# Turning the attention probabilities of eight token tiles by four 128x128 transposes each, with v laid out key by key

## The chip, the cores and the metric

The kernel runs on one core of a Trainium2 chip. The metric is device time in microseconds of one execution. Five engines work side by side, each through its own list of instructions in order: TensorE (PE: matrix products and transposes into PSUM), VectorE (DVE), ScalarE (ACT), GpSimd (POOL) and SyncE (SP), which here only issues DMAs. An engine that must wait for another's result holds up everything behind it in its list.

## The reference

Two steps on 4608 tokens. Attention inside chunks of 64 tokens, for 8 batches, 8 heads of 64 features and 9 chunks per sequence of 576:

```python
scores = scale * np.matmul(q_c, k_c.transpose(0, 1, 2, 4, 3))
scores = scores - np.max(scores, axis=-1, keepdims=True)
attn = np.exp(scores)
attn = attn / (np.sum(attn, axis=-1, keepdims=True) + 1e-09)
out = np.matmul(attn, v_c)
```

The heads of a token are then laid side by side to 512 features x, and

```python
h = x @ w_in                      # 512 -> 2048
g = np.where(h > 0.0, h, np.exp(np.minimum(h, 0.0)) - 1.0)
return g @ w_out                  # 2048 -> 512
```

The weights `w_in` and `w_out` arrive as float64 and are rebuilt on the chip into a high and a low part, so that three products of reduced precision stand for one product of full precision.

## The kernel before, in words

Tokens are worked in blocks of 512, a block in four token tiles of 128. A token tile is two chunks of 64 tokens, c = 0 and 1, on the 128 partitions. The first three blocks ("plain") use weights held on the chip; the remaining six go in pairs with fewer products, ordered by a planner, and the change does not touch them.

Attention of the first eight token tiles goes through `early_attention` (line 264), a generator whose steps other work is put between: q and k of the tile are transposed on PE in four 128x128 pieces each (L270) and copied to SBUF by ACT (L277); 16 small products per tile give the scores (L248), each on a 64x64 quarter of the array; DVE takes the maximum per head (L283) and subtracts it (L299), ACT takes exp (L303), DVE sums and divides (L305 to L308). Three of the eight tiles (2, 4 and 5, `BY_HEAD`) have exp and sum on ACT head by head instead (L293). Then the probabilities `a` (128 tokens by 8 heads of 64 keys) must be turned so that keys lie on partitions: before, 16 matmuls against 64x64 corners of the identity, one per head and chunk (L315). ACT copies the result (L322) and 16 small products with v give x (L256). Half of the array serves chunk 0, half chunk 1: `v_sb` holds the 64 tokens of chunk 0 on partitions 0 to 63 with all 8 heads, and of chunk 1 on partitions 64 to 127. One DMA loads it (`load_heads`, L206), or two where the tile's chunks belong to two batches (tile 4).

Tiles 0 to 3 are worked ahead of everything by a written list of items, `START`: `q0`, `k0`, `v0` are loads, `u0`, `u1`, ... loads of a weight unit (`load_unit`, L118 and L125; a unit u is 128 columns of `w_in` and, from u1 on, 128 rows of `w_out`), `0` to `3` the next step of that tile, `r` and `d` steps of the rebuilding of a unit on ACT (L139, L144, L179) and DVE (L161, L168, L172, L185). Units arrive in three buffers `st`. Tiles 4 to 7 are worked inside the first block by a second list, `FIRST_BLOCK`, between its 16 rounds: `H` is 12 products into `h` (L434; L451 in the first round), `e` the steps of the elu (ACT L468, L469, L476; DVE L471, L479), `P` 12 products into `o`, `L4` to `L7` the loads of a token tile and `4` to `7` its steps. The rebuilding of units 3 to 16 runs in the same list, so DVE and ACT rebuild the weights just ahead of the products that use them.

SP issues every load in the order of these lists. The framework gives DMAs eight semaphores in turn, and a DMA waits until the eighth DMA before it has landed.

Of the kernel before, what the change touches and what calls it, by code (L numbers as in the profile page):

```python
# [10 lines left out]
F32 = mybir.dt.float32  # L11
# [4 lines left out]
ALU = mybir.AluOpType  # L16
# [4 lines left out]
def kernel(  # L21
# [181 lines left out]
    def load_heads(src, name: str, n0: int, pool):  # L203
# [4 lines left out]
            )  # L208
        return dst

    U = 4

    def load_tokens(n0: int, qk):
# [39 lines left out]
    def multiply_v(x_ps, v_sb, aT):  # L253
        for hp in range(NK):
            for c, j in quarters:
                nc.tensor.matmul(  # L256
                    x_ps[halves[j], c, hp, :], lhsT=v_sb[halves[c], 2 * hp + j, :],
                    rhs=aT[halves[c], :, j * NK + hp], start=True, stop=True,
                )

    def first_halves(pair_of_banks):
        return pair_of_banks[:, :, :NK * C].rearrange("p i (h t) -> p i h t", h=NK)

    def early_attention(tt: int, q_sb, k_sb, get_v, kT, at, a_pool, get_banks, put, by_head: bool):


        both = get_banks()
        for i, src in enumerate((q_sb, k_sb)):
            for hp in range(NK):
                nc.tensor.transpose(  # L270
                    out=both[:, i, hp * P:(hp + 1) * P], in_=src[:, 2 * hp:2 * hp + 2, :],
                    identity=ident,
                )
# [11 lines left out]
        a_heads = a.rearrange("p (j h) t -> p j h t", j=2)  # L285
        z = sm.tile([P, 2, NK, 1], F32, name="z")
        if by_head:

            nc.vector.tensor_scalar_mul(mx, mx, -SCALE)
            yield  # L290
            for j in range(2):
                for h in range(NK):
                    nc.scalar.activation(  # L293
                        out=a_heads[:, j, h, :], in_=scores[:, j, h, :], func=AF.Exp, scale=SCALE,
                        bias=mx[:, j, h, :], accum_out=z[:, j, h, :],
                    )
            yield
        else:
            nc.vector.tensor_tensor(  # L299
                out=a_heads, in0=scores, in1=mx.broadcast_to([P, 2, NK, C]), op=ALU.subtract  # L300
            )
            yield
            nc.scalar.activation(out=a, in_=a, func=AF.Exp, scale=SCALE)  # L303
            yield
            nc.vector.tensor_reduce(out=z, in_=a_heads, axis=AX.X, op=ALU.add)  # L305
        nc.vector.tensor_scalar_add(z, z, 1e-9)
        nc.vector.reciprocal(z, z)
        nc.vector.tensor_tensor(  # L308
            out=a_heads, in0=a_heads, in1=z.broadcast_to([P, 2, NK, C]), op=ALU.mult
        )  # L310
        yield
        turned_ps = both[:, 0, :].rearrange("p (h t) -> p h t", h=H)
        for h in range(H):
            for half in halves:
                nc.tensor.matmul(  # L315
                    turned_ps[half, h, :], lhsT=a[half, h, :], rhs=ident[half, half],
                    start=True, stop=True,
                )
        yield

        aT = at.tile([P, NK, P], F32, name="qT").rearrange("p h (j t) -> p (h j) t", j=2)
# [92 lines left out]
    def by_chunk(x, ts):  # L414
        return x[:, :, ts].rearrange("p h (c t) -> p c h t", c=2)

    def keep_x(n: int, src):
        half = (n // NTT + 1) % 2 if n >= PLAIN * NTT else 0
        ts = slice(n % NTT * P, (n % NTT + 1) * P)
        nc.scalar.copy(out=by_chunk(xf[:, half], ts), in_=src)  # L420

    def split_first_x(tt: int, src):
        ts = slice(tt * P, (tt + 1) * P)
        hi = by_chunk(xhi, ts)
        nc.scalar.copy(out=hi, in_=src)
        nc.vector.tensor_tensor(
            out=by_chunk(xlo, ts), in0=src, in1=hi.bitcast(F32), op=ALU.subtract)

# [698 lines left out]
    with (  # L1127
        tc.tile_pool(name="start", bufs=NTT) as start,
        tc.tile_pool(name="ps_start", bufs=NTT, space=bass.MemoryType.PSUM) as ps_start,
    ):  # L1130
        make_identity(nc, ident)
        loaded, tiles, warmed = {}, {}, []

        def start_banks():
            return ps_start.tile([P, 2, DM], F32, name="ps_a")

        def start_step(item: str):
            tt = int(item)
            if tt not in tiles:
                tiles[tt] = early_attention(  # L1140
                    tt, *[loaded[kind, tt] for kind in "qk"], lambda: loaded["v", tt],
                    start.tile([P, NK, P], F32, name="kT"), start, start,
                    lambda: start_banks() if tt else warmed[0],
                    split_first_x, tt in BY_HEAD)
            next(tiles[tt])

        for item in START.split():
            kind, n = item[0], item[1:]
            if kind == "w":
                warm(int(n))  # L1150
            elif kind == "u":
                load_unit(int(n))
            elif kind in "qkv":
                loaded[kind, int(n)] = load_heads(
                    {"q": q, "k": k, "v": v}[kind], f"{kind}_sb", int(n) * P, start)
# [31 lines left out]
    def early_tile(n: int):  # L1187

        n0 = n * P
        heads = [io[:, 2 * (n % 2) + i, :].rearrange("p (h d) -> p h d", h=H) for i in range(2)]  # L1190
        loaded = [load_heads(src, name, n0, pool)
                  for src, name, pool in ((q, "q_sb", heads[0]), (k, "k_sb", heads[1]), (v, "v_sb", vio))]
        q_sb, k_sb, v_sb = loaded
        return early_attention(
            n % NTT, q_sb, k_sb, lambda: v_sb, k_turned, at, wi1,
            lambda: ps_early.tile([P, 2, DM], F32, name="ps_a"),
            lambda tt, src: keep_x(tt, src), n in BY_HEAD)

    def place_of_tokens(n: int):

# [744 lines left out]
```

## Time and profile before

| | us |
|---|---|
| median of 3 runs (lowest, highest) | 826.16 (824.86, 826.62) |
| span of the profiled execution, first to last instruction | 823.4 |
| what lies around the span, median less span | 2.8 |

| engine | busy us | share of the span |
|---|---|---|
| PE | 804.4 | 98% |
| DVE | 613.1 | 74% |
| ACT | 523.5 | 64% |
| POOL | 171.1 | 21% |

The profiled execution has no time of its own beside its span; the median of the runs stands for it. Busy shares are averages over stages with different limits. The stage before the first product of the first block lasts 28.9 us, the first block about 100 us, and what the change does lies in these two. A duration in a row includes a little of the next instruction's start, so the distance between the starts of two rows in a row is the cost of the first.

### The profile page before, as it was taken

The numbers are of one execution on the slowest core, as the hardware profiler recorded it, in microseconds if no ns is written. First come the engines' busy times: TensorE is split into PE (matmuls) and PEld (weight loads), VectorE is DVE, ScalarE is ACT, GpSimd is POOL, SyncE is SP. The second block draws the span as 40 slices with busy tenths as digits, with TensorE's granted clock in tenths as the row PEclk, the third lists the DMA queues.
The fourth block names the chain that finished last, engine by engine and source line by source line (L and its number), as shares of the span: only waits on it lengthen the run. The fifth ranks groups of instructions, "written<-read, shape, count | busy, mean of one in ns | idle before, by whom it ended". The sixth has DMA issues, their size and how long they took to land.

```text
span 823.4 us, 15851 instructions
## 1 busy us (share of the span) xinstructions
PE 804.4 (98%) x5853; PEld 655.6 (80%) x5853; DVE 613.1 (74%) x914; ACT 523.5 (64%) x990; POOL 171.1 (21%) x149
## 2 busy tenths in 40 slices
PE   6799999999999999999999999999999999999997
PEld 5688878888778878878888888778788888888885
DVE  4999997666776659767656867868889956557964
ACT  5999885544554546766666445888867737776451
POOL 0000014264525531443111254000020100000100
PEclk9999999999999999999999999999999999999999
DMA  9976994889778887689986789999876585566755
GB/s 234 272 212 209 270 328 130 244 243 267 219 215 231 231 269 205 202 241 281 283 235 188 218 246 299 286 322 287 249 204 206 195 269 193 193 196 190 226 186 149
DMA packets 183229, 191.90 MB, mean 233 GB/s; under 512 B 84720, under 2 KB 151792, under 8 KB 183152
## 3 DMA queue, kind: packets, MB, share of 16 engines
q1 hardware_dynamic: 182512, 188.80, 77.2%
q0 software_dynamic: 640, 2.10, 0.6%
q8 instruction: 46, 0.75, 0.4%
q14 instruction: 31, 0.25, 0.1%
HBM read 144.18 MB, written 42.99 MB: 227 GB/s over the span
## 4 chain that ended last, share of the span: by engine, by line
PE 83%; DMA 8%; SPq 3%; ACT 2%; DVE 2%; issue 1%; DVEq 0%; ACTq 0%
PE o L434 43%; PE h L434 34%; DMA ring<-a_dram 3%; PE ps_a L248 2%; PE ps_a L256 2%; SPq L206 2%; PE h L451 1%; DMA st<-in_moe_w_out_dram 1%; DMA kept<-in_k_dram 1%; DMA a_dram<-wi_lo 1%; DMA kept<-in_q_dram 1%; DMA a_dram<-wi_hi 1%; DMA v_sb<-in_v_dram 1%; PE ps_a L315 1%; DMA ring<-w_dram 1%
## 5 line engine op out<-in xcount | busy, mean ns | idle before, releaser
L434 PE MATMUL o<-wo_hi,ghi 128*128 128x512 f32 x272 | 107.6, 396 | 0.0
L434 PE MATMUL o<-wo_hi,glo 128*128 128x512 f32 x272 | 106.1, 390 | 0.3 <-DVE glo L479 0.3
L434 PE MATMUL o<-wo_lo,ghi 128*128 128x512 f32 x272 | 106.0, 390 | 0.0
L434 PE MATMUL h<-xhi,wi_hi 128*128 128x512 f32 x228 | 84.0, 397 | 0.1
L434 PE MATMUL h<-xlo,wi_hi 128*128 128x512 f32 x228 | 82.3, 390 | 0.0
L434 PE MATMUL h<-xhi,wi_lo 128*128 128x512 f32 x180 | 70.3, 390 | 0.0
L434 PEld LDWEIGHTS o<-wo_hi,glo 128*128 128x128 f32 x272 | 51.1, 188 | 11.7 <-DVE glo L479 0.7
L434 PEld LDWEIGHTS o<-wo_hi,ghi 128*128 128x128 f32 x272 | 51.0, 188 | 11.1
L434 PEld LDWEIGHTS o<-wo_lo,ghi 128*128 128x128 f32 x272 | 51.1, 188 | 10.2
L510 POOL TENSOR_TENSOR kept<-wi_hi,wi_lo 128x512 f32<-128x512 f32 x16 | 21.7, 1376 | 158.8 <-DVE xf L172 118.2
L471 DVE SCALAR_TENSOR_TENSOR e<-e,h 128x512 f32<-128x512 f32 x48 | 32.8, 684 | 25.2 <-ACT e L469 24.8
L434 PE MATMUL o<-split,ring 128*128 128x512 f32 x216 | 51.0, 390 | 0.0
L434 PEld LDWEIGHTS h<-xhi,wi_hi 128*128 128x128 f32 x228 | 42.6, 188 | 9.8 <-ACT kept L785 0.8
L434 PEld LDWEIGHTS h<-xlo,wi_hi 128*128 128x128 f32 x228 | 42.8, 188 | 8.5
L434 PEld LDWEIGHTS o<-split,ring 128*128 128x128 f32 x216 | 40.5, 188 | 8.4
L393 ACT COPY unturned<-turned 128x512 f32<-128x512 f32 x28 | 17.4, 621 | 46.0 <-DVE turned L388 37.9
L468 ACT ACTIVATE e<-h 128x512 f32<-128x512 f32 x48 | 28.6, 596 | 25.0 <-PE h L434 22.5
L476 ACT CAST ghi<-e 128x512 fp32r<-128x512 f32 x48 | 29.8, 621 | 19.8 <-DVE e L471 19.6
L746 POOL TENSOR_TENSOR glo<-e,ghi 128x512 fp32r<-128x512 f32 x16 | 20.7, 1296 | 96.9 <-ACT ghi L744 96.9
L434 PE MATMUL h<-split,ring 128*128 128x512 f32 x168 | 40.3, 391 | 0.0
L1492 ACT ACTIVATE e<-e 128x512 f32<-128x512 f32 x64 | 39.5, 630 | 1.0
L434 PEld LDWEIGHTS h<-xhi,wi_lo 128*128 128x128 f32 x180 | 33.8, 188 | 7.5 <-DVE wi_lo L185 0.4
(225 smaller groups left out, 2011.3 us busy)
## 6 DMA issues: line engine op xcount, KB each, us to landing
ring<-a_dram SPq DMA_DIRECT2D x56, 512.0 KB, 5.3
ring<-w_dram SPq DMA_DIRECT2D x56, 512.0 KB, 4.3
wi_hi<-a_dram SPq DMA_DIRECT2D x56, 256.0 KB, 5.3
kept<-in_q_dram SPq DMA_DIRECT2D x100, 128.0 KB, 3.8
kept<-in_k_dram SPq DMA_DIRECT2D x100, 128.0 KB, 4.0
wo_lo<-lo_dram SPq DMA_DIRECT2D x20, 512.0 KB, 5.8
v_sb<-in_v_dram SPq DMA_DIRECT2D x32, 256.0 KB, 5.4
st<-in_moe_w_in_dram SPq DMA_DIRECT2D x16, 512.0 KB, 4.9
```

The source lines that it names most:

```text
L206: nc.sync.dma_start(out=dst[p0:p0 + n], in_=src[b, :, s0:s0 + n, :].rearrange("h s d -> s h d"))
L248: nc.tensor.matmul(scores[halves[c], j, hp, :], lhsT=qT[halves[j], hp, halves[c]], rhs=kT[halves[j], hp, halves[c]], start=True, stop=True,)
L256: nc.tensor.matmul(x_ps[halves[j], c, hp, :], lhsT=v_sb[halves[c], 2 * hp + j, :], rhs=aT[halves[c], :, j * NK + hp], start=True, stop=True,)
L315: nc.tensor.matmul(turned_ps[half, h, :], lhsT=a[half, h, :], rhs=ident[half, half], start=True, stop=True,)
L393: nc.scalar.copy(out=unturned, in_=turned)
L434: nc.tensor.matmul(ps, lhsT=a, rhs=b, start=start, stop=stop, skip_group_check=onto)
L468: nc.scalar.activation(out=e, in_=h, func=AF.Relu, scale=-1.0)
L471: nc.vector.scalar_tensor_tensor(out=e, in0=e, scalar=-1.0, in1=h, op0=ALU.add, op1=ALU.max)
L476: nc.scalar.copy(out=ghi, in_=e)
L510: nc.gpsimd.tensor_tensor(out=out, in0=a, in1=b, op=op)
L746: engine.tensor_tensor(out=lo, in0=e, in1=hi.bitcast(F32), op=ALU.subtract)
L1492: nc.scalar.activation(out=units[u], in_=units[u], func=AF.Exp, scale=-1.0)
```

## The change

The probabilities of a head pair (2 heads of 64 keys) are turned by one 128x128 transpose, so a tile takes 4 of them in place of 16 matmuls. After it the keys of one head of the pair lie on partitions 0 to 63 and those of the other on 64 to 127, with the tokens of both chunks beside each other. So the half of the array is now chosen by the head (r = head // 4), not by the chunk, and v must lie to match: `load_v_by_key` loads four pieces of 64 keys by 4 heads, one for each r and chunk c, with a DMA each. The heads are stored in `a` in the order (j, b, r), head = 4r + 2b + j; that order does not fit one DVE instruction, so the subtraction of the maximum becomes two instructions of half the size (in the five tiles that are not `BY_HEAD`). The x that results is laid out by bank instead of by chunk, and is read by ACT and DVE at the same sizes as before. `START` and `FIRST_BLOCK` are unchanged.

```diff
+    def load_v_by_key(n0: int, pool):
+        dst = pool.tile([P, 2, NK, D], F32, name="v_sb")
+        for r in range(2):
+            for c in range(2):
+                b, s0 = divmod(n0 + c * C, S)
+                nc.sync.dma_start(
+                    out=dst[halves[r], c],
+                    in_=v[b, r * NK:(r + 1) * NK, s0:s0 + C, :].rearrange("h s d -> s h d"))
+        return dst
...
+    def multiply_v_by_key(x_ps, v_sb, aT):
+        for c in range(2):
+            for b in range(2):
+                for r, j in quarters:
+                    nc.tensor.matmul(
+                        x_ps[halves[j], r, b, halves[c]], lhsT=v_sb[halves[r], c, 2 * b + j, :],
+                        rhs=aT[halves[r], 2 * j + b, halves[c]], start=True, stop=True,
+                    )
...
-            nc.vector.tensor_tensor(
-                out=a_heads, in0=scores, in1=mx.broadcast_to([P, 2, NK, C]), op=ALU.subtract
-            )
+            for j in range(2):
+                nc.vector.tensor_tensor(
+                    out=a_heads[:, j], in0=scores[:, j].rearrange("p (r b) t -> p r b t", r=2),
+                    in1=mx[:, j].rearrange("p (r b) e -> p r b e", r=2).broadcast_to([P, 2, 2, C]),
+                    op=ALU.subtract)
...
-        turned_ps = both[:, 0, :].rearrange("p (h t) -> p h t", h=H)
-        for h in range(H):
-            for half in halves:
-                nc.tensor.matmul(
-                    turned_ps[half, h, :], lhsT=a[half, h, :], rhs=ident[half, half],
-                    start=True, stop=True,
-                )
+        turned_ps = both[:, 0, :].rearrange("p (h t) -> p h t", h=NK)
+        for h in range(NK):
+            nc.tensor.transpose(out=turned_ps[:, h, :], in_=a[:, 2 * h:2 * h + 2, :], identity=ident)
...
-        x_ps = first_halves(both)
-        multiply_v(x_ps, get_v(), aT.rearrange("p h (u t) -> p u h t", u=2))
+        x_ps = both[:, :, :NK * C].rearrange("p r (b t) -> p r b t", b=2)
+        multiply_v_by_key(x_ps, get_v(), aT)
```

On SP, the loads at the start, from k of tile 3 on, before (`DMAHW0` to `DMAHW7` are the eight semaphores in turn, each row waits for the load that used it last):

```order
L206 DMA k_sb<-in_k_dram 128x8x64 [waits DMAHW0_49]
L206 DMA v_sb<-in_v_dram 128x8x64 [waits DMAHW1_49]
L206 DMA v_sb<-in_v_dram 128x8x64 [waits DMAHW2_49]
L206 DMA v_sb<-in_v_dram 128x8x64 [waits DMAHW3_49]
L118 DMA st<-in_moe_w_in_dram 128x4x256 [waits DMAHW4_49]
L118 DMA st<-in_moe_w_in_dram 128x4x256 [waits DMAHW5_49]
L125 DMA st<-in_moe_w_out_dram 128x1024 [waits DMAHW6_49]
```

and after, from the second half of the v of tile 2 on; k of tile 3 is the load that used `DMAHW3` last:

```order
L218 DMA v_sb<-in_v_dram 64x4x64 [waits DMAHW2_49]
L218 DMA v_sb<-in_v_dram 64x4x64 [waits DMAHW3_49]
L218 DMA v_sb<-in_v_dram 64x4x64 [waits DMAHW4_49]
L218 DMA v_sb<-in_v_dram 64x4x64 [waits DMAHW5_49]
L218 DMA v_sb<-in_v_dram 64x4x64 [waits DMAHW6_49]
L218 DMA v_sb<-in_v_dram 64x4x64 [waits DMAHW7_49]
L118 DMA st<-in_moe_w_in_dram 128x4x256 [waits DMAHW0_49]
L118 DMA st<-in_moe_w_in_dram 128x4x256 [waits DMAHW1_49]
L125 DMA st<-in_moe_w_out_dram 128x1024 [waits DMAHW2_49]
```

The weight units stand behind 16 loads of v (tiles 0 to 3) where they stood behind 4.

On PE, the turning of tile 4's probabilities in the first block, before (`o_508` is the accumulator of the fourth token tile of the block):

```order
L434 MATMUL o_508<-wo_lo,ghi 128x512
L434 MATMUL o_508<-wo_hi,glo 128x512
L315 MATMUL ps_a<-ident,a 64x64 x16
L434 MATMUL h<-xhi,wi_hi 128x512
L434 MATMUL h<-xlo,wi_hi 128x512
L434 MATMUL h<-xhi,wi_lo 128x512
```

and after:

```order
L457 MATMUL o_475<-wo_lo,ghi 128x512
L457 MATMUL o_475<-wo_hi,glo 128x512
L341 MATMUL ps_a<-ident,a 128x128 x4
L457 MATMUL h<-xhi,wi_hi 128x512
L457 MATMUL h<-xlo,wi_hi 128x512
L457 MATMUL h<-xhi,wi_lo 128x512
```

The place among the products is the same; 4 instructions stand where 16 stood, here and for tiles 5, 6 and 7.

## Rows read from the trace of the kernel before

**Rows 1.** The page, part 4: the chain that ended last, by engine

```profile
PE 83%; DMA 8%; SPq 3%; ACT 2%; DVE 2%; issue 1%; DVEq 0%; ACTq 0%
```

**Rows 2.** That chain in order of time: start, us, what

```profile
14.86 7.24 DMA st<-in_moe_w_out_dram
...
28.89 3.02 PE h L451 x12
...
41.81 2.72 PE o L434 x12
44.53 1.08 PE ps_a L315 x32
45.60 2.95 PE h L434 x12
...
52.13 0.87 PE ps_a L270 x8
53.01 2.73 PE h L434 x12
```

**Rows 3.** Busy by stretch: us, PE, PEld, DVE, ACT, POOL, clock, DMA share, GB/s

```profile
28.90:121.00 92.10, 92.10 (x753) 74.12 (x754) 87.42 (x123) 83.11 (x151) 1.39 (x2) 1.00 0.83 254
...
105.40:121.40 16.00, 16.00 (x126) 12.51 (x124) 15.60 (x23) 13.54 (x23) 1.79 (x2) 1.00 1.02 337
```

**Rows 4.** SP in order of time: start, us, DMAs issued

```profile
9.25 4.16 SPq L206 DMA_DIRECT2D v_sb<-in_v_dram  x3
115.19 1.76 SPq L227 DMA_DIRECT2D kept<-in_q_dram  x4
```

**Rows 5.** DMA issues from 0.7, 8.0, 11.3, 14.9: count, size, us to landing

```profile
q_sb<-in_q_dram SPq DMA_DIRECT2D x1, 256.0 KB, 3.0
...
k_sb<-in_k_dram SPq DMA_DIRECT2D x1, 256.0 KB, 5.5
...
v_sb<-in_v_dram SPq DMA_DIRECT2D x1, 256.0 KB, 4.8
...
st<-in_moe_w_out_dram SPq DMA_DIRECT2D x1, 512.0 KB, 7.2
```

**Rows 6.** Busy time by stretch, the end of the q and k loads

```profile
13.00:15.00 2.00, 1.28 (x36) 0.98 (x36) 0.06 (x1) 0.79 (x2) 0.00 (x0) 1.00 0.76 174
```

**Rows 7.** ACT in order of time: start, us, instruction [idle before, released by]

```profile
22.19 1.11 ACT L139 ACTIVATE st<-st 128x1024 f32<-128x1024 f32 x1 [0.86 <-DMA st<-in_moe_w_out_dram]
...
102.15 1.17 ACT L139 ACTIVATE st<-st 128x1024 f32<-128x1024 f32 x1 [1.01 <-DMA st<-in_moe_w_out_dram]
...
103.67 0.60 ACT L277 COPY k_turned<-ps_a 128x512 f32<-128x512 f32 x1
```

**Rows 8.** DVE in order of time, the same columns

```profile
61.87 0.69 DVE L283 TENSOR_REDUCE mx<-ps_a 128x8 f32<-128x512 f32 x1 [0.41 <-PE ps_a L248]
...
68.80 0.69 DVE L471 SCALAR_TENSOR_TENSOR e<-e,h 128x512 f32<-128x512 f32 x1 [0.92 <-ACT e L469]
...
105.46 0.69 DVE L471 SCALAR_TENSOR_TENSOR e<-e,h 128x512 f32<-128x512 f32 x1 [1.00 <-ACT e L469]
...
120.09 1.29 DVE L185 TENSOR_TENSOR wi_lo<-xf,wi_hi 128x512 fp32r<-128x512 f32 x1
```

**Rows 9.** DVE by line and shape: count, busy us, mean ns

```profile
L299 DVE TENSOR_TENSOR a<-ps_a,mx 128x512 f32<-128x512 f32 x5 | 3.5, 691 | 0.2
L720 DVE TENSOR_TENSOR xf<-xf 128x256 f32<-128x256 f32 x8 | 3.3, 416 | 0.1
```

**Rows 10.** The chain again, end of the first block

```profile
104.35 0.66 PE ps_a L248 x32
...
118.31 5.72 PE h L434 x24
```

**Rows 11.** PE in order of time, the start: start, us, instruction [idle before]

```profile
4.19 1.06 PE L270 MATMUL ps_a<-ident,q_sb 128*128 128x128 f32 x4
...
5.89 0.68 PE L270 MATMUL ps_a<-ident,q_sb 128*128 128x128 f32 x4
```

More of the change, by code (lines that the diff above doesn't have):

```diff
@@ L259, in multiply_v, with by_bank @@
                 )
+    def multiply_v_by_key(x_ps, v_sb, aT):
[6 more added lines that the diff above has]
+                    )
+    def by_bank(x, ts):
+        return x[:, :, ts].rearrange("p (r b) t -> p r b t", r=2)
     def first_halves(pair_of_banks):
@@ L284, in early_attention @@
         a = a_pool.tile([P, H, C], F32, name="a")
-        a_heads = a.rearrange("p (j h) t -> p j h t", j=2)
-        z = sm.tile([P, 2, NK, 1], F32, name="z")
+        a_heads = a.rearrange("p (j b r) t -> p j r b t", j=2, b=2)
+        z = sm.tile([P, H, 1], F32, name="z")
+        z_heads = z.rearrange("p (j b r) e -> p j r b e", j=2, b=2)
         if by_head:
@@ L293, in early_attention @@
                     nc.scalar.activation(
-                        out=a_heads[:, j, h, :], in_=scores[:, j, h, :], func=AF.Exp, scale=SCALE,
-                        bias=mx[:, j, h, :], accum_out=z[:, j, h, :],
+                        out=a_heads[:, j, h // 2, h % 2, :], in_=scores[:, j, h, :], func=AF.Exp, scale=SCALE,
+                        bias=mx[:, j, h, :], accum_out=z_heads[:, j, h // 2, h % 2, :],
                     )
@@ L304, in early_attention @@
             yield
[L305 removed]
+            nc.vector.tensor_reduce(out=z, in_=a, axis=AX.X, op=ALU.add)
         nc.vector.tensor_scalar_add(z, z, 1e-9)
         nc.vector.reciprocal(z, z)
[L308 to L310 removed]
+        nc.vector.tensor_tensor(out=a, in0=a, in1=z.broadcast_to([P, H, C]), op=ALU.mult)
         yield
[L312 to L318 removed]
+        turned_ps = both[:, 0, :].rearrange("p (h t) -> p h t", h=NK)
+        for h in range(NK):
+            nc.tensor.transpose(out=turned_ps[:, h, :], in_=a[:, 2 * h:2 * h + 2, :], identity=ident)
         yield
[L321 removed]
+        aT = at.tile([P, NK, P], F32, name="qT")
         nc.scalar.copy(out=aT, in_=turned_ps)
         yield
[L324 to L325 removed]
+        x_ps = both[:, :, :NK * C].rearrange("p r (b t) -> p r b t", b=2)
+        multiply_v_by_key(x_ps, get_v(), aT)
         yield
@@ L415, in by_chunk, with keep_x @@
         return x[:, :, ts].rearrange("p h (c t) -> p c h t", c=2)
-    def keep_x(n: int, src):
+    def keep_x(n: int, src, of=by_chunk):
         half = (n // NTT + 1) % 2 if n >= PLAIN * NTT else 0
         ts = slice(n % NTT * P, (n % NTT + 1) * P)
-        nc.scalar.copy(out=by_chunk(xf[:, half], ts), in_=src)
+        nc.scalar.copy(out=of(xf[:, half], ts), in_=src)
     def split_first_x(tt: int, src):
         ts = slice(tt * P, (tt + 1) * P)
-        hi = by_chunk(xhi, ts)
+        hi = by_bank(xhi, ts)
         nc.scalar.copy(out=hi, in_=src)
         nc.vector.tensor_tensor(
-            out=by_chunk(xlo, ts), in0=src, in1=hi.bitcast(F32), op=ALU.subtract)
+            out=by_bank(xlo, ts), in0=src, in1=hi.bitcast(F32), op=ALU.subtract)
     def three(ps, a_hi, a_lo, b_hi, b_lo, start, stop, onto=False):
@@ L1152 @@
                 load_unit(int(n))
-            elif kind in "qkv":
-                loaded[kind, int(n)] = load_heads(
-                    {"q": q, "k": k, "v": v}[kind], f"{kind}_sb", int(n) * P, start)
+            elif kind == "v":
+                loaded[kind, int(n)] = load_v_by_key(int(n) * P, start)
+            elif kind in "qk":
+                loaded[kind, int(n)] = load_heads({"q": q, "k": k}[kind], f"{kind}_sb", int(n) * P, start)
             elif kind == "r":
@@ L1191, in early_tile @@
         loaded = [load_heads(src, name, n0, pool)
-                  for src, name, pool in ((q, "q_sb", heads[0]), (k, "k_sb", heads[1]), (v, "v_sb", vio))]
-        q_sb, k_sb, v_sb = loaded
+                  for src, name, pool in ((q, "q_sb", heads[0]), (k, "k_sb", heads[1]))]
+        q_sb, k_sb = loaded
+        v_sb = load_v_by_key(n0, vio)
         return early_attention(
```

2 lines of the change are left out of this document (1 added, 1 removed).

## The prediction, made before the change was run

> **What bounds the kernel now.** I read the page's chain first: 83% of it is PE [rows 1], so after the start the kernel is a string of matmuls. Then that chain in order of time. It has two parts that the change touches. Up to 28.89 us it is not PE's: it runs through SP's issues of q, k and v, then the landing of the first `w_out` rows (issued 14.86, landed 7.24 later), and from there through ACT, which begins to rebuild them at 22.19, to the first product at 28.89 [rows 2, 7]. From 28.89 on it is PE without a gap. In the stretch from 28.9 to 121 PE is busy 92.1 of 92.1 us, but DVE is too for 87.42 and ACT for 83.11, and the DMA engines for 0.83 of it [rows 3]. So in the first block PE ends last, with three others close behind; that is what decides how much of a faster PE is kept.
>
> **The change part by part.**
>
> *PE, first block.* The 16 matmuls of a tile cost 1.08 us from the start of the first to the start of what follows, and the 12 products behind them cost 2.95, where 12 such products behind 12 others cost 2.72 [rows 2]: together 4.03. Eight 128x128 transposes cost 0.87, and the 12 products behind those 2.73 [rows 2]. Four should cost half, 0.44, so 3.17 in all. That is 0.86 saved per tile, and four tiles lie in this block: 3.44 us on PE. The 16 products with v keep number and shape.
>
> *How much of it is kept.* PE may move ahead only as far as the operands are there earlier. The tightest place is near the end of the block. At 102.15 ACT has stood 1.01 us waiting for the weights of a unit, and the copy of k for tile 7, two instructions later (103.67, some 0.60 long, so 104.27), is used by PE at 104.35 [rows 7, 10]: 0.08 us of slack. From 105.46, after its own idle 1.00 behind that same ACT work, DVE runs nearly without a gap (busy 15.6 of the 16.0 us from 105.4 on [rows 3]) up to a weight's low part that ends at 120.09 + 1.29 = 121.38 [rows 8]. The third product of the second group of 12 in the row at 118.31 needs it, at 118.31 + 5.72 / 2 + 0.45 = 121.62 [rows 10]: 0.24 of slack. So at 121 PE is early by at most 0.24 plus whatever that late weight unit is early. The unit's buffer is freed by DVE, and DVE can only be early through the idle it has: 0.41 at 61.87 behind PE's scores and 0.92 at 68.80 behind an ACT step that itself waits for PE [rows 8]. At 68.80 PE has one turned tile behind it, so 0.86 is what these two can give.
>
> *DVE, the split subtraction.* One instruction of 691 ns becomes two of half the size. The nearest row of that size has 416 ns, so 2 x 416 - 691 = 141 ns more per tile [rows 9]. Tiles 0, 1 and 3 pay in the start, where DVE waits for scores and has room; 6 and 7 pay in the first block, on the DVE string just described: 0.28 us. Summed: 0.86 - 0.28 + 0.24 = 0.8 us kept. The ends are 0 (the late unit does not move at all, the slack goes to the two splits) and 3.44 (all of them move along). I take 0.8, since it is the one that the slack rows give.
>
> *SP and the DMAs, start.* A v load of 256 KB becomes four of 64 KB. SP took 4.16 us for the last three v loads, held by what was still in flight; the shortest pitch in the trace for small loads is 1.76 / 4 = 0.44 us [rows 4], so 4 x 0.44 = 1.76 per tile. The wait on the eighth load before matters more: the last quarter of tile 2's v now waits for k of tile 3 (issued 8.00, landed 5.5 later [rows 5], at 13.5), and four quarters of tile 3 stand behind it. The first weight unit is then issued at 13.5 + 5 x 0.44 = 15.7 where it was issued at 9.25 + 4.16 + 0.05 = 13.46: 2.24 later. What is queued behind on SP is units 0, 1 and 2, and for them ACT waits, last at 22.19 [rows 7], then DVE, then PE at 28.89. The cover is the backlog of the DMA engines: before, the last v landed at 11.34 + 4.8 = 16.1 [rows 5]. Now its last quarter is issued at 15.3 and lands about 2.25 later (an estimate: the first load's 3.0 [rows 5] less the 0.75 that three quarters of its bytes take at the pace of about 1 us per load), at 17.5: 1.4 later, and the weights are behind it in the same engines. Against this, the engines have spare time right there (busy 0.76 from 13 to 15 [rows 6]), so the backlog gives back a part. I take +1.1 us; the ends are 0 (hidden wholly) and +2.5 (the 2.24, and a pitch of 0.05 more for each of five quarters). From 22.19 to 28.89 ACT has no gap to absorb it, so it goes through one for one.
>
> *The rest of the start.* PE turns tiles 0 to 3 faster too, some 0.6 us each, but the chain there is DMA and ACT [rows 2]: nothing. In the first block tiles 4 to 7 also take four v loads each; SP stands mostly behind full queues or waiting for buffers there, and v is what a tile needs last: 0, with 0.3 at the upper end, which I leave to the +2.5.
>
> *A rule that speaks against it.* Four transposes of q take 1.06 us at 4.19 and 0.68 at 5.89, and up to there PE had done nothing but transposes (`warm` and L270) [rows 11]; the granted clock of the first block reads 1.00, the 2.4 GHz level [rows 3]. The Trainium skill (TensorE: Matmul & The Clock Gate, Part 4: PE-mode transpose) says that the full clock does not engage for transposes, as they do not count as busy in the same way. By that rule, putting 16 transposes for 64 matmuls in the start could let the clock fall before 28.89; by the rows, transposes alone were enough for it to speed up, so the sum stays as it is.
>
> The Trainium skill also says (DMA: Bandwidth & Descriptors, Rules for kernel authors) that two transfers to disjoint partition halves gain nothing over one of 128 partitions; no row here shows v loaded in quarters, and the sum goes by the pitch above.
>
> **The sum.** Span 823.4 + 1.1 - 0.8 = 823.7; the 2.8 us between span and median bring it to 826.5, against a median of 826.16.
>
> **The rivals.**
>
> *PE's saving is kept whole.* For it: PE shows no wait at all in the block, and ACT and DVE themselves wait for PE in places (0.41, and part of the 0.92 [rows 8]), so a faster PE pulls them along; the late weight unit may be early too. Against: 87.42 us of DVE work in 92.1 leave only 4.7, spread out. Then 823.4 + 1.1 - 3.4 = 821.1 of span, 823.9; with the start's delay hidden as well, 822.8.
>
> *The weights come later than the backlog hides, and nothing is kept.* For it: eight loads in flight are now often eight times 64 KB, so the DMA engines can run dry between 13.5 and 18; the chain crosses exactly these loads. Against: the engines were not full there before either (0.76 [rows 6]), so part of that dry spell is already in the 22.1. It decides if the `w_out` rows land after 23.8 in place of 22.1. Then 823.4 + 2.5 - 0 = 825.9, so 828.7.
>
> *The clock falls.* PE's work in the start shrinks, and the first 12 products at 28.89 run at the half level: 3.02 more [rows 2], beside the +1.1 and -0.8, so 829.5. Against: the granted clock stayed at 1.00 with PE idle for a third of the stretch from 13 to 15 [rows 6]. The skill's rule above is the reason to keep it at all.
>
> **How the numbers follow.** What can be told from no change is about 0.2%, 1.65 us. Forecast, delay and saving near cancelling: 0.47, all but 0.01 of it within that bound. Saving kept: 0.24, faster. Weights late: 0.26, slower. Clock: 0.03, slower. So faster 0.25, same 0.46, slower 0.29. The range that holds 8 in 10 reaches from 823.6 to 828.7, into both outer cases; the forecast's own range is 825.0 to 827.7.
>
> **What would show it.** Right: the four transposes of a tile at some 0.44 in the chain, and 2.73 behind them; ACT's L139 row of 22.19 later by about 1; the first product at about 30; PE's scores of tile 7 later than 104.35 or within 0.5 of it, with new waits of PE for DVE or ACT inside the block. Wrong: the first product at 28.9 or earlier, or PE without waits and the last product of the block over 2 us earlier (then the slack I read was not the limit), or weights landing after 23.8.

## The result, and the profile of the changed kernel

| | before | changed |
|---|---|---|
| median of the runs on one chip, us | 826.18 (824.86 to 826.62) | 833.94 (833.08 to 835.28) |
| ratio, 95% interval | | 1.0091 (1.0067 to 1.0114) |
| span of the profiled execution, us | 823.4 | 831.3 |
| mean granted clock of the profiled execution | 0.999 | 0.985 |

The changed kernel is 0.9% slower, and 833.94 lies 5.2 us above the upper end of the range.

SP in order of time, the start of the changed kernel (start, us, DMAs issued; answers to [rows 4]):

```profile
3.62 3.40 SPq L218 DMA_DIRECT2D v_sb<-in_v_dram  x4
...
10.26 9.42 SPq L218 DMA_DIRECT2D v_sb<-in_v_dram  x12
...
12.47 1.93 SPq L218 DMA_DIRECT2D v_sb<-in_v_dram  x3
...
19.72 1.15 SPq L118 DMA_DIRECT2D st<-in_moe_w_in_dram  x2
```

A quarter of v costs SP 0.85 us on average in the first row and 9.42 / 12 = 0.79 in the second. The first quarter of each group takes longer, 1.42 at 3.62 and 2.17 at 10.26, where the DMA engines were full (share 1.0 and more); whether that is the reason was not tried. Behind it the issues follow each other at about 0.66, as the third row, a cut-out of the second, has it (three loads with 1.93 in all). The first weight unit, issued at 13.46 before, goes out at 19.72: 6.26 later.

ACT in order of time (start, us, instruction, idle before and what ended it; answers to [rows 7]):

```profile
24.71 0.65 ACT L139 ACTIVATE st<-st 128x512 f32<-128x512 f32 x1 [4.57 <-DMA st<-in_moe_w_in_dram]
27.38 1.14 ACT L139 ACTIVATE st<-st 128x1024 f32<-128x1024 f32 x1
...
109.60 1.14 ACT L139 ACTIVATE st<-st 128x1024 f32<-128x1024 f32 x1 [2.38 <-DMA st<-in_moe_w_out_dram]
```

The rebuild that stood at 22.19 starts at 27.38, since ACT waited 4.57 for the first weight unit. The late unit near the end of the block comes later too: ACT waits 2.38, where it waited 1.01.

Busy time by stretch (columns as in [rows 3]; the clock stands ahead of the DMA share; the first row answers to [rows 6]):

```profile
13.00:15.00 2.00, 1.29 (x7) 1.05 (x8) 0.01 (x1) 0.51 (x1) 0.00 (x0) 0.83 0.48 108
15.00:20.00 5.00, 3.88 (x75) 2.80 (x73) 3.15 (x8) 3.40 (x18) 0.00 (x0) 0.73 0.43 98
20.00:25.00 5.00, 1.12 (x5) 0.71 (x4) 1.69 (x5) 0.43 (x3) 0.00 (x0) 0.61 0.86 263
25.00:30.00 5.00, 2.63 (x67) 2.45 (x68) 4.17 (x8) 5.00 (x10) 0.00 (x0) 0.50 0.95 345
30.00:35.00 5.00, 3.61 (x69) 2.79 (x68) 4.56 (x7) 5.00 (x7) 0.00 (x0) 0.50 0.86 245
110.00:115.00 5.00, 3.27 (x40) 2.67 (x41) 2.63 (x6) 4.37 (x9) 0.00 (x0) 0.83 1.06 387
...
34.00:129.00 95.00, 92.64 (x640) 74.28 (x641) 87.55 (x125) 83.33 (x152) 1.44 (x2) 0.96 0.79 247
```

Two things are to be seen. The DMA engines are busy for only 0.43 of the time from 15 to 20, while SP is issuing without a pause: they stand idle for want of issues (a quarter issued there lands in a median of 2.5 us). And the granted clock, 1.00 in the rows of before, is 0.50 (the 1.2 GHz level) from 25 to 35, and 0.83 on average from 110 to 115. From 20 to 25, where it settles at the lower level, PE is busy 1.12 of 5 us. The last row is the whole first block and answers to [rows 3]: PE is busy 92.64 of 95.00 us.

PE in order of time, the first products and the turning of tile 4:

```profile
34.06 2.08 PE L474 MATMUL h<-xhi,wi_hi 128*128 128x512 f32 x4 [0.88 <-ACT xhi L448]
35.94 1.91 PE L474 MATMUL h<-xhi,wi_lo 128*128 128x512 f32 x4
37.64 1.36 PE L474 MATMUL h<-xlo,wi_hi 128*128 128x512 f32 x4
38.84 1.04 PE L296 MATMUL ps_a<-ident,io 128*128 128x128 f32 x8
...
51.51 0.60 PE L341 MATMUL ps_a<-ident,a 128*128 128x128 f32 x4
51.86 0.48 PE L457 MATMUL h<-xhi,wi_hi 128*128 128x512 f32 x1
...
54.80 0.40 PE L279 MATMUL ps_a<-qT,v_sb 64*64 64x64 f32 x12
...
111.73 0.69 PE L260 MATMUL ps_a<-k_turned,qT 64*64 64x64 f32 x32 [2.13 <-ACT k_turned L303]
```

The first 12 products start at 34.06, 5.17 after the 28.89 of [rows 2], and take 38.84 - 34.06 = 4.78 us against 3.02 there. The turning and the 12 products behind it take 54.80 - 51.51 = 3.29, against 4.03 of before. At 111.73 PE stands 2.13 for the copy behind the late unit, where it did not wait at all.

How far the changed kernel lies behind, step by step, is read from the DVE steps of the elu, which both kernels have at the same places. Four of before (start, us):

```profile
33.30 0.69 DVE L471 SCALAR_TENSOR_TENSOR e<-e,h 128x512 f32<-128x512 f32 x1
...
98.73 0.68 DVE L471 SCALAR_TENSOR_TENSOR e<-e,h 128x512 f32<-128x512 f32 x1
...
110.36 0.68 DVE L471 SCALAR_TENSOR_TENSOR e<-e,h 128x512 f32<-128x512 f32 x1
```

(the fourth, at 105.46, is in [rows 8]), and the same four of the changed kernel:

```profile
40.39 0.69 DVE L494 SCALAR_TENSOR_TENSOR e<-e,h 128x512 f32<-128x512 f32 x1 [0.72 <-ACT e L492]
...
104.81 0.68 DVE L494 SCALAR_TENSOR_TENSOR e<-e,h 128x512 f32<-128x512 f32 x1
112.88 0.69 DVE L494 SCALAR_TENSOR_TENSOR e<-e,h 128x512 f32<-128x512 f32 x1 [2.33 <-ACT e L492]
118.30 0.69 DVE L494 SCALAR_TENSOR_TENSOR e<-e,h 128x512 f32<-128x512 f32 x1 [0.38 <-ACT e L492]
```

It is 7.09 behind at the first step, 6.08 at the one of 98.73, 7.42 at 105.46 and 7.94 at 110.36; the spans differ by 7.9. So the account is: 5.17 up to the first product, from later weights; 1.92 up to the first step, of which 4.78 - 3.02 = 1.76 is the products at the half clock; -1.01 gained by the faster turning; and 1.86 lost at the late unit and behind it. Below, "behind at the first, second and last step" means these three places (33.30, 98.73, 110.36 of before), read the same way.

### The profile page after: what moved, and what is told of

It is laid out like the page before. It is cut to its first block, busy times and chain, and to the rows that moved or that the text cites. A ratio compares the mean times of both kernels' runs of the same rounds, so it can differ in the third digit from the quotient of the medians.

```text
span 831.3 us, 15425 instructions
## 1 busy us (share of the span) xinstructions
PE 806.4 (97%) x5629; PEld 656.1 (79%) x5629; DVE 614.3 (74%) x919; ACT 523.5 (63%) x990; POOL 171.1 (21%) x149
## 5 line engine op out<-in xcount | busy, mean ns | idle before, releaser
L494 DVE SCALAR_TENSOR_TENSOR e<-e,h 128x512 f32<-128x512 f32 x48 | 32.8, 684 | 26.9 <-ACT e L492 26.7
L491 ACT ACTIVATE e<-h 128x512 f32<-128x512 f32 x48 | 28.7, 598 | 26.7 <-PE h L457 23.5
```

Of the source, the lines that this page charges most:

```text
L491: nc.scalar.activation(out=e, in_=h, func=AF.Relu, scale=-1.0)
L494: nc.vector.scalar_tensor_tensor(out=e, in0=e, scalar=-1.0, in1=h, op0=ALU.add, op1=ALU.max)
```

## The experiments

Each kernel was timed beside the kernel before on its chip. "Clock" is the mean granted clock of whole executions: 74 executions of before have 0.992 to 1.000, mean 0.996; the changed kernel's four have 0.982 to 0.988. "Behind" compares one profile of each kernel with the one profile of before, whose 0.999 is among its highest clocks. Three kernels below leave the start as it was, and their profiles are 0.1, 0.9 and 1.2 behind at the first step; so differences of about 1 us in that column show nothing by themselves.

| kernel | us | ratio to before, 95% | clock, mean of n | behind at first, second, last step, us |
|---|---|---|---|---|
| changed | 833.94 | 1.0091 (1.0067 to 1.0114) | 0.985 of 4 | 7.1, 6.1, 7.9 |
| quarters_alone | 836.65 | 1.0126 (1.0099 to 1.0153) | 0.988 of 4 | 7.3, 7.4, 11.6 |
| transposes_alone | 829.12 | 1.0029 (1.0012 to 1.0046) | 0.990 of 12 | 1.3, 0.3, 2.9 |
| v_after_weights | 833.27 | 1.0085 (1.0061 to 1.0109) | 0.987 of 6 | 5.9, 4.9, 6.3 |
| quarters_128_partitions | 832.54 | 1.0079 (1.0059 to 1.0100) | 0.992 of 4 | 2.4, 4.5, 4.8 |
| transposes_padded | 827.54 | 1.0016 (0.9998 to 1.0034) | 0.997 of 12 | -0.6, -1.1, 0.1 |
| six_matmuls | 827.12 | 1.0005 (0.9984 to 1.0027) | 0.990 of 12 | 1.0, 0.1, 0.3 |
| v_on_gpsimd | 854.91 | 1.0348 (1.0320 to 1.0376) | 0.974 of 4 | 28.5, 27.5, 26.7 |
| new_in_block_only | 829.52 | 1.0042 (1.0024 to 1.0060) | 0.994 of 12 | 1.2, 0.2, 2.9 |
| start_filled | 837.25 | 1.0116 (1.0090 to 1.0141) | 0.991 of 5 | 5.2, 4.2, 7.3 |
| v01_on_act | 832.12 | 1.0065 (1.0042 to 1.0089) | 0.989 of 12 | 4.4, 3.4, 6.3 |
| block_unit14_early | 827.28 | 1.0000 (0.9980 to 1.0020) | 0.996 of 12 | 0.9, 0.0, 0.3 |
| before_unit14_early | 826.00 | 0.9993 (0.9971 to 1.0015) | 0.996 of 12 | 0.1, 0.7, 0.6 |

### Which half of the change costs

**quarters_alone.** The kernel before, with each v load of the eight tiles cut in four.

```diff
+        for r in range(2):
+            for c in range(2):
+                b, s0 = divmod(n0 + c * C, S)
+                nc.sync.dma_start(
+                    out=dst[c * C:(c + 1) * C, r * NK:(r + 1) * NK],
+                    in_=v[b, r * NK:(r + 1) * NK, s0:s0 + C, :].rearrange("h s d -> s h d"))
```

> The kernel before, with matmuls turning the probabilities as there, and only the v loads of the eight tiles cut into four pieces of 64 partitions by 4 heads. Theory 1 (the quarter loads are the whole loss: SP needs about 0.66 us for each, the weights are issued late, PE idles and its clock falls): the first weight unit is issued near 19.7 in place of 13.46, the first product stands near 34, the granted clock falls to half between about 14 and 38, and the time is 834 to 836 (the changed kernel's 833.9 without the 1 us that the transposes give back). Theory 2 (transposes in place of matmuls let the clock fall): the clock stays at 1.00, the weights are late all the same, and the time is at most 831.5.

```profile
10.45 9.14 SPq L216 DMA_DIRECT2D v_sb<-in_v_dram  x12
19.63 1.16 SPq L118 DMA_DIRECT2D st<-in_moe_w_in_dram  x2
```

SP's rows start where those of the changed kernel do, within 0.3 us, and with the 16 matmuls unchanged the kernel is as far behind at the first step (7.3). It does not catch up by the second, where the changed kernel gained 1.0. The quarter loads alone make the loss of the start, and they bring the low clock with them (0.50 from 25 to 35). The time, 836.65, lies a little above theory 1's range, for the quarters cost again in the block: those of tile 7 stand just ahead of the late unit on SP,

```profile
99.27 5.88 SPq L216 DMA_DIRECT2D v_sb<-in_v_dram  x4
```

5.88 for them, where the one load of before took 3.24. The `w_out` rows of the unit go out at 106.33, 9.20 later than before in a kernel that is 7.4 behind, ACT waits 4.83 for them and PE 3.72 behind it, and 4.3 more is lost by the last step.

**transposes_alone.** The kernel before, with whole v loads and one subtraction, turned by four transposes.

```diff
-        for h in range(H):
-            for half in halves:
-                nc.tensor.matmul(
-                    turned_ps[half, h, :], lhsT=a[half, h, :], rhs=ident[half, half],
-                    start=True, stop=True,
-                )
+        for h in range(NK):
+            nc.tensor.transpose(
+                out=both[:, 0, h * P:(h + 1) * P], in_=a[:, 2 * h:2 * h + 2, :], identity=ident)
```

> The kernel before with whole v loads and its one subtraction, and only the 16 matmuls of each of the eight tiles replaced by four 128x128 transposes; the layouts then do not fit each other, so x of these eight tiles is not the reference's. Theory 1: the clock stays at 1.00 throughout, the first product stays at 28.9, and PE keeps about 1.0 us (0.86 plus the 0.24 of slack, without the cost of the split subtraction) by the end of the first block: 824.8 to 825.6. Theory 2: the clock falls at the start as in the changed kernel and the first products run at half speed: 828 or more. If all the PE saving is kept: 822.7.

The gain that theory 1 expected did not come; theory 2's 828 or more did. Busy by stretch:

```profile
20.00:25.00 5.00, 4.37 (x96) 3.55 (x98) 4.59 (x9) 4.45 (x8) 0.00 (x0) 0.50 0.97 334
...
105.00:110.00 5.00, 3.37 (x39) 2.69 (x40) 2.19 (x4) 4.43 (x9) 0.00 (x0) 0.78 1.07 385
```

With SP as before, the clock is at half by 20 to 25, and falls once more at 105 to 110 behind a wait of PE. The gain from first to second step is 1.0, as in the changed kernel; it is lost again, and more, by the last step. Its 1.3 at the first step is no more than a kernel with the start of before can show (1.2 in new_in_block_only); what sets it apart is the mean clock of 12 executions, 0.990 against 0.996.

### What in the quarter loads costs

**v_after_weights.** The changed kernel with the v loads of `START` behind unit 1.

```diff
-        "... w13 v0 0 1 0 q2 0 k2 q3 0 k3 1 1 v1 0 2 v2 1 3 0 2 2 v3 1 2 3 u0 3 1 2 u1 0 "
+        "... w13 0 1 0 q2 0 k2 q3 0 k3 1 1 0 2 1 3 0 2 2 1 2 3 u0 3 1 2 u1 v0 v1 v2 v3 0 "
```

> The changed kernel with one edit in the written list of the start: the v loads of tiles 0 to 3 stand behind the loads of weight units 0 and 1 instead of ahead of them; v stays in quarters. Theory 1: units 0 and 1 are issued from about 9.3 on, the first product returns to 28 to 29.5, the clock stays at 1.00 at the start, and what remains is about 1 us of saving on PE against up to 1.9 us that the late unit near 102 costs in the first block: 824 to 827. Theory 2: the 64 matmuls are still missing from the start, the clock falls there, 829 or more.

```profile
9.99 14.29 SPq L218 DMA_DIRECT2D v_sb<-in_v_dram  x16
24.32 0.60 SPq L118 DMA_DIRECT2D st<-in_moe_w_in_dram  x1
```

Unit 0 goes out at 7.92, but the 16 loads now hold back unit 2 until 24.32, and 5.9 us are lost at the first step. The delay moved with the loads. Theory 1's 824 to 827 was missed, and 833.27 is where theory 2 put it; but the weights came late again (the first product stands at 32.50 behind a wait of PE of 5.69) and the clock was at half from 20 to 35, so this kernel does not tell the theories apart.

**quarters_128_partitions.** Quarters of 128 partitions by 2 heads in place of 64 by 4, else as quarters_alone.

```diff
+        for i in range(4):
+            heads_of = slice(2 * i, 2 * i + 2)
+            for p0, b, s0, n in pieces_of(n0, 1):
+                nc.sync.dma_start(
+                    out=dst[p0:p0 + n, heads_of],
+                    in_=v[b, heads_of, s0:s0 + n, :].rearrange("h s d -> s h d"))
```

> The kernel before with the v loads of the eight tiles cut into four pieces of the same 64 KB, but each of 128 partitions by 2 heads. If the count of DMAs is what costs (each issue about 0.66 us, or the wait on the eighth load before): as the quarters of 64 partitions, first weight unit issued near 19.7, 834 to 836. If it is the shape of 64 partitions: SP takes 0.4 to 0.45 for each, the first weight unit is issued near 15.7 as the prediction had it, the first product 0 to 2.5 later than 28.9, and the time is 826 to 829.

```profile
9.88 7.49 SPq L216 DMA_DIRECT2D v_sb<-in_v_dram  x12
17.41 1.02 SPq L118 DMA_DIRECT2D st<-in_moe_w_in_dram  x2
```

7.49 / 12 = 0.62 per load, against 0.76 in quarters_alone; where issue follows issue it is 0.51 against 0.66. Neither forecast came. The first weight unit is 3.95 later than before in place of 6.17, so by the issue the count is the larger part and the shape the smaller. At the first step this profile is only 2.4 behind, against 7.3, with the first product at 31.22 and its 12 products at the full clock.

**v_on_gpsimd.** The changed kernel with the quarters issued by GpSimd.

```diff
-                nc.sync.dma_start(
+                nc.gpsimd.dma_start(
```

> The changed kernel with all v quarters of the eight tiles issued from GpSimd's queue, so SP's list is that of before without its v loads. Theory 1 (SP's issue of 16 small loads ahead of the weights is what delays them): the first weight unit is issued at 10 or earlier, ACT does not wait over 1 us for it, the first product starts at 28 to 30, and the time is 826 to 830, the upper part if the clock falls as with the transposes alone. Rival (the DMA engines are slower with 64 KB pieces, whoever issues them): the landing of the weights stays 3 us or more late and the time is 831 to 835.

The first half of theory 1's expectation came: unit 0 was issued at 8.30, and ACT rebuilt it at 17.20 without a wait. The time did not: GpSimd's own issues are far apart,

```profile
16.67 0.63 POOL L218 DMA_DIRECT2D v_sb<-in_v_dram  x1 [6.40 <-issue]
20.72 0.62 POOL L218 DMA_DIRECT2D v_sb<-in_v_dram  x1 [3.43 <-issue]
```

and PE waits for v. The time lies far above both forecasts and tells the theories apart no further; the rival's late landing of the weights did not come.

**v01_on_act.** The changed kernel, v of tiles 0 and 1 from ScalarE's queue.

```diff
+                loaded[kind, int(n)] = load_v_by_key(int(n) * P, start, nc.scalar if int(n) < 2 else nc.sync)
```

> The changed kernel with the v quarters of tiles 0 and 1 issued from ScalarE's queue, at times when ScalarE has nothing to do; SP issues 8 quarters at the start in place of 16. Theory 1 (the number of loads on SP ahead of the weights): SP reaches the first weight unit at 13 to 15, the first elu step is 0.5 to 3 us later than before (the clock may still fall, as with the transposes alone), and the time is 827 to 830.5. Rival (the DMA engines take longer for v in pieces of 64 KB, whoever issues them): the weights land as late as in the changed kernel, first elu step 5 or more later, 832 or more.

Theory 1 missed: SP reached the weights at 16.75, not 13 to 15, and the time is at the rival's 832, though the first step is 4.4 behind and not 5 or more. ACT's rows show one reason:

```profile
6.66 5.17 ACTq L218 DMA_DIRECT2D v_sb<-in_v_dram  x3
11.87 0.59 ACT L303 COPY qT<-ps_a 128x512 f32<-128x512 f32 x1 [5.04 <-DMA v_sb<-in_v_dram]
```

ACT stood 5.2 us in three issues, with the copies for all tiles behind them. What held these issues was not tried: the eight semaphores taken in turn, or the DMA engines, which were full up to 10. Moving loads to another engine moved the wait to that engine.

### What makes the clock fall

**transposes_padded.** As transposes_alone, with 10 transposes per tile, 6 of them repeats.

```diff
-        for h in range(NK):
+        for h in (0, 1, 2, 3, 0, 1, 0, 1, 2, 3):
```

> The kernel before with whole v loads and one subtraction, as in transposes_alone, but each tile's turning is 10 transposes (6 of them repeat a piece) in place of 4, so that PE spends about the 1.08 us that the 16 matmuls took; x of the eight tiles is not the reference's. Theory 1 (the clock falls in the start because PE has less to do there): the granted clock stays at full from 19 to 33, the first elu step on DVE is within 0.4 of before, and the time is 825.5 to 827. Theory 2 (it falls because transposes don't hold it as matmuls do): half from about 19 to 33 as with 4 transposes, first elu step 1.3 later or more, 828.5 to 831.

**six_matmuls.** The kernel before with 6 of the 16 turning matmuls.

```diff
-        for h in range(H):
+        for h in (0, 1, 2):
```

> The kernel before with only 6 of the 16 turning matmuls of a tile (about 0.41 us in place of 1.08, like four transposes); the other ten pieces keep what lay there, so x of the eight tiles is not the reference's. Theory 1 (less to do): the clock falls in the start as in transposes_alone, half from about 19 to 33, and the time is 828 to 830. Theory 2 (the kind of instruction): the clock stays full there, the saving of 0.67 per tile shows up to 99 us as in transposes_alone, and the time is 824.5 to 826.5.

Busy by stretch, first of transposes_padded, then of six_matmuls:

```profile
20.00:25.00 5.00, 2.75 (x102) 2.33 (x91) 3.95 (x8) 4.17 (x7) 0.00 (x0) 1.00 0.98 348
```

```profile
20.00:25.00 5.00, 3.74 (x108) 3.40 (x108) 4.53 (x9) 4.82 (x8) 0.00 (x0) 0.50 0.96 339
...
105.00:110.00 5.00, 5.00 (x46) 4.04 (x38) 4.10 (x8) 4.41 (x9) 0.00 (x0) 1.00 1.08 387
```

Over 12 executions each the pattern is plain: 4 transposes and 6 matmuls have the same clock, 0.990; 10 transposes have 0.997, as before's 16 matmuls (0.996). So the mean clock went with how much PE was given to do in the turnings, not with the kind of instruction. A single profile does not show this: before_unit14_early, with all 16 matmuls and the start of before, reads 0.54 from 15 to 20, and block_unit14_early 0.76 from 20 to 25. In time theory 1 was less exact: transposes_padded ended 0.5 above its range, six_matmuls 0.9 below, since its 1.0 at the first step was paid back by the faster turning up to the second (0.1), and since it lost only 0.3 from there to the last step, where transposes_alone lost 2.5.

**start_filled.** The changed kernel with transposes of the identity where PE waits in the start.

```diff
+            for i in range((8, 8, 30, 6)[tt]):
+                nc.tensor.transpose(out=both[:, 1, (2 + i % 2) * P:(3 + i % 2) * P], in_=ident, identity=ident)
```

> The changed kernel with 52 transposes of the identity put into a free part of PSUM behind the turning of tiles 0 to 3 (8, 8, 30 and 6), where PE stands waiting; results are those of the changed kernel. Theory 1 (the later weights cost about 5.2 us by themselves, and the rest of the 7.1 lost by the first elu step is the clock, which fell because PE had little to do): the clock stays full up to the first product, that starts at 33.5 to 34.5, its 12 products take about 3.0, the first elu step is 5.0 to 5.6 later than before, and the time is 831 to 833. Rival (the clock falls there whatever PE does while it waits, or transposes don't hold it): half over 21 to 38 as in the changed kernel, 833.5 or more.

PE in order of time, and busy by stretch:

```profile
33.75 1.20 PE L477 MATMUL h<-xhi,wi_hi 128*128 128x512 f32 x4 [1.33 <-ACT xhi L451]
```

```profile
15.00:20.00 5.00, 4.90 (x82) 4.27 (x81) 2.74 (x7) 2.95 (x15) 0.00 (x0) 0.59 0.43 97
...
25.00:30.00 5.00, 3.35 (x85) 3.05 (x84) 4.48 (x9) 5.00 (x9) 0.00 (x0) 1.00 0.98 346
...
250.00:255.00 5.00, 3.16 (x72) 2.41 (x71) 1.72 (x2) 1.82 (x3) 2.45 (x2) 0.96 0.61 154
```

The clock did fall, to 0.59 from 15 to 20, most of it ahead of the first added transposes, which stand at 19.05; but with them it was back at full from 20 on and stayed there, where the changed kernel has 0.50 to 0.61 from 20 to 35. From there theory 1 was met: first product at 33.75, its 12 products in 2.86, 5.24 behind at the first step, so by these two profiles the clock's share of the 7.09 is 1.85. The total was not: 837.25, above the changed kernel and in the rival's range. In the profile it is 7.3 behind at the last step, and loses 3 us more near 253, in a stretch that the change doesn't touch, where PE waits 1.84 for a load. Why the later blocks give this kernel a new wait is open.

### What takes the gain in the block

**new_in_block_only.** Tiles 0 to 3 as before, tiles 4 to 7 as changed.

```diff
-                tiles[tt] = early_attention(
+                tiles[tt] = first_attention(   # the function of before, with whole v loads
```

> Tiles 0 to 3 as before the change (whole v load, 16 matmuls), tiles 4 to 7 as changed. Theory 1 (the loss arises in the start): the start is as before, first elu step within 0.2 of before; the saving grows to about 1.0 us by 99 us as it did in the other runs. Behind that the late weight unit at 105 decides: 824.5 to 826 if the clock stays full from 105 to 121, 826 to 828.5 if it falls there again as in the changed kernel and in transposes_alone. Rival (the quarter loads in the first block cost as much as those in the start): 829 or more.

**block_unit14_early.** The same, with unit 14 issued right behind the v of tile 7.

```diff
-        "6 e e r d s l2 L7 e r r H d e 6 d d l3 s u14 6 d s u15 ...
+        "6 e e r d s l2 L7 u14 e r r H d e 6 d d l3 s 6 d s u15 ...
```

> As new_in_block_only, and the loads of unit 14 are issued right behind the v of tile 7, one store earlier than before. Theory 1 (in the block the faster turning is turned into a longer wait for this unit at 102, and PE's wait there lets the clock fall): ScalarE waits under 1 us for the unit, the clock stays full from 105 to 115 in most executions, and the time is 825 to 827.5, at least 2 us under new_in_block_only. Rival (something else in the block costs the time, as the quarter loads on SP or the second subtraction): 829 or more, though the unit is earlier.

**before_unit14_early.** The kernel before with this one move.

> The kernel before with the loads of unit 14 issued right behind the v of tile 7, one store earlier. Theory 1: its wait of 1.0 at 102 goes, but what PE needs next has only 0.1 to 0.3 us of slack on DVE and ScalarE, so 825.5 to 827, the same within 0.2%. Rival (the late unit already holds the kernel before): 1 us or more under the kernel before in the same call.

ACT's wait for the unit and the stretch behind it, in new_in_block_only:

```profile
104.57 1.14 ACT L139 ACTIVATE st<-st 128x1024 f32<-128x1024 f32 x1 [3.21 <-DMA st<-in_moe_w_out_dram]
```

```profile
105.00:110.00 5.00, 3.29 (x38) 2.69 (x39) 2.11 (x5) 4.37 (x9) 0.00 (x0) 0.71 1.05 382
```

and in block_unit14_early:

```profile
102.41 1.15 ACT L139 ACTIVATE st<-st 128x1024 f32<-128x1024 f32 x1 [1.30 <-DMA st<-in_moe_w_out_dram]
```

```profile
105.00:110.00 5.00, 5.00 (x40) 3.97 (x30) 4.20 (x9) 4.35 (x9) 0.00 (x0) 1.00 1.08 383
```

With the start of before, the first step of new_in_block_only was still 1.2 behind in its profile, though nothing in the list of PE, ACT or DVE is changed there: the clock reads 0.86 from 25 to 30 and 0.80 from 30 to 35 in that execution, and executions of before have falls too (mean 0.996, not 1). That part of the expectation was missed, and the time of 829.52 is above the range and in the rival's, 829 or more. Against the rival speak two kernels. block_unit14_early keeps the quarter loads in the block and both subtractions, and has a ratio of 1.0000 in place of 1.0042 with the unit issued 1.1 earlier (96.75 in place of 97.86); ACT's wait there is 1.30, not the under 1 expected. And transposes_alone, without quarter loads, loses as much from the second to the last step (2.5) as new_in_block_only (2.7). So the quarter loads are not needed for this loss, though they add to it where they hold the unit back, as in quarters_alone. In before the same move changes nothing that can be told from no change: ACT's wait goes from 1.01 to 0.81, not away. So in the block the gain is first turned into a longer wait for this unit, and behind PE's wait of 2.13 in the changed kernel, and of 2.70 to 3.72 in five others, the clock falls. It need not: in v_after_weights PE waits 2.11 there and the clock reads 1.00 from 105 to 120. When the unit lands isn't set by its issue alone: issues of its `w_out` rows from 94.77 (transposes_padded) to 97.86 were first used by ACT between 102.2 and 104.6, in stretches where the DMA engines are about full (share 0.93 to 1.04 from 100 to 105); what orders them was not tried.

No version here beats the kernel before.

## Why the prediction was wrong, by its steps

**The start, the step that failed first.** "I take +1.1 us; the ends are 0 and +2.5." It was 5.17 to the first product. The pitch was wrong: 0.44 came from the loads of [rows 4] in 32 partitions, while quarters of v followed each other at 0.66, and at 0.51 in their best shape. A nearer row was there to be read: before loads q and k of tile 4 in halves of 64 partitions, and SP's row for them is

```profile
23.32 1.41 SPq L206 DMA_DIRECT2D io<-in_q_dram  x2
```

0.70 for a load. At 0.70 the sixteen quarters cost 11.2 in place of the 0.85 (issued at 3.93) + 4.16 of four whole loads, 6.2 more, beside the 6.26 measured. That it comes out so near is partly luck: the quarters took 3.40 + 9.42 = 12.82, with the slow first ones, and the loads of q and k between them went out some 1.5 faster than before. The sum also counted only five quarters behind a wait for k of tile 3, and none of the eleven before them; tile 0's four alone pushed q of tile 2 back from 4.83 to 7.06. So the upper end was no bound: it assumed that SP's time was hidden up to 13.5 by what it waited for, and SP itself was the limit (DMA share 0.43 from 15 to 20).

**"The clock falls", at 0.03.** All four executions have a low mean clock, 0.982 to 0.988. Its price of 3.02 was the full half-speed price of the 12 products; 1.76 was paid, since the clock rose again before the last of them (1.36 for the last four, against 2.08 for the first). What spoke against it, the clock at 1.00 with PE idle a third of 13 to 15 [rows 6], was two microseconds of one execution, whose 0.999 was near the top of what before's executions have. The rule in the Trainium skill (TensorE: Matmul & The Clock Gate, Part 4: PE-mode transpose), that transposes do not count as busy in the same way, gave the right warning for another reason than the runs show: 10 transposes kept the clock as 16 matmuls did, and 6 matmuls lost it as 4 transposes did.

**PE's saving per tile.** 0.86 predicted, 4.03 - 3.29 = 0.74 measured: right. The four transposes took 0.35, not 0.44, and the products behind them 2.94, not 2.73.

**"0.8 us kept."** 1.01 was kept up to 98.73, near the 0.86 that the prediction gave to two waits of DVE. That it is near is luck. Of the two only the 0.41 at 61.87 is gone; the 0.92 at 68.80 is still there,

```profile
75.24 0.69 DVE L494 SCALAR_TENSOR_TENSOR e<-e,h 128x512 f32<-128x512 f32 x1 [0.93 <-ACT e L492]
```

and the rest came from waits that it did not name, 0.34 at 49.89, of which 0.16 is left, and 0.27 at 92.68. Then the step that the low end held, "the late unit does not move at all", came about and more: ACT used the unit 7.45 later than before, in a kernel that was 6.08 behind, and 1.86 went. The 0.24 of slack behind it played no part, since PE now waited ahead of it, at the scores of tile 7, where the prediction had read 0.08.

**The split subtraction.** The mean of one half is as the prediction took it, but its cost is not:

```profile
L327 DVE TENSOR_TENSOR a<-ps_a,mx 128x256 f32<-128x256 f32 x10 | 3.8, 420 | 0.2
```

```profile
114.20 0.76 DVE L327 TENSOR_TENSOR a<-ps_a,mx 128x256 f32<-128x256 f32 x2
114.87 0.68 DVE L502 TENSOR_TENSOR glo<-e,ghi 128x512 fp32r<-128x512 f32 x1
```

420 ns stands beside the 416 of [rows 9], so the difference of durations would be 149 ns per tile. But durations overlap. From start to start the two halves of tile 7 cost 114.87 - 114.20 = 0.67, where the one instruction of before cost 0.61 (106.78 to 107.39), and tile 6 has the same: 0.06 per tile and 0.12 for the two, in place of 0.28. The term was mis-sized, by too little to matter beside 5.17.

**The rivals.** "The weights come later" had the right mechanism with a price of 2.5 that was half of what it cost, and "the clock falls" was held to be a case by itself. In the changed kernel they come together: later weights leave PE standing, and the clock is low there; quarters_alone, with late weights and all 16 matmuls, has 0.988, and transposes_alone, with the weights on time, 0.990. Taken together and at the measured sizes, 823.4 + 5.2 + 1.9 - 1.0 + 1.9 = 831.4.

## What to carry to other kernels

Cutting a load in pieces costs issue time on the queue for every piece; where the queue also carries what the chain waits for, count all pieces ahead of it, at the pitch of the row nearest in shape, 0.70 in this case and not 0.44, and look whether the queue or the DMA engines are the limit. Work taken off PE ahead of a wait can cost more than it gives: in transposes_alone PE stood longer at the late unit, the mean clock was 0.990 against 0.996, and the kernel was 0.3% slower, not faster. The cost of an instruction in a list without gaps is read from start to start, not from its duration. A granted clock read from one execution is a sample; the mean over many executions is what to reason from.

## What was not expected of the hardware

- Where issue followed issue, a load of 64 KB took SP 0.51 us in 128 partitions and 0.66 in 64; the first whole v load, 256 KB, took 0.85 in before and 1.00 in transposes_alone. The Trainium skill (DMA: Bandwidth & Descriptors, Rules for kernel authors) says that two transfers to disjoint partition halves gain nothing over one of 128 partitions; here quarters of 64 partitions cost 7.3 us at the first step, in quarters_alone, and quarters of 128 partitions 2.4.
- On GpSimd's queue quarter loads of v followed each other at 2.5 to 7 us in the start.
- The granted clock read 0.83 from 110 to 115 behind PE's wait of 2.13, in a block in which PE was otherwise busy almost throughout; in new_in_block_only it read 0.71 from 105 to 110, behind a wait of 2.95 at the same instruction. In block_unit14_early, with a wait of 1.07, it read 1.00, and in v_after_weights, with one of 2.11, too.
